# The first product of a mixture-of-experts layer in 26 block products instead of 28, with its operands kept in DRAM

## The chip, the core and the metric

One core of a Trainium2 chip runs the whole program. The metric is device time in microseconds from the start to the end of one execution; shown are the median of the runs and, beside it, one execution that was profiled. PE is the matrix engine (PEld its weight loads), DVE the vector engine, ACT the scalar engine, POOL GpSimd, SP the engine that issues most DMAs.

## The reference, cut to what matters

```python
# chunked attention over q, k, v (4 x 8 x 768 x 64) gives x, 3072 tokens of 512
def _moe_ref(x, w_gate, w1, w2):
    ...                              # P: 3072 x 8, a softmax normalised 8 times over rows and columns
    for e in range(E):               # 8 experts
        h = np.maximum(x @ w1[e], 0.0)      # 512 -> 1024
        ye = h @ w2[e]                      # 1024 -> 512
        out += P[:, e:e + 1] * ye
    return out.astype(np.float32)
```

All is float32, and every token goes through every expert.

## The kernel before, in words

**Tiling.** The tokens are cut in six *units* of 512, each in two halves of 256 (`GT`). The program goes through 48 pairs of expert and unit, `units[n]`: expert 0 on its six units, then expert 1 backwards, and so on. For each pair there is a *first product* (`hidden`, L1616), `h = relu(x @ w1)`, and a *second* (`output`, L1867), `h @ w2`, scaled by the routing weight and added to a running output.

**Number format.** Each float32 operand is scaled by a power of two and split in a high and a low float16 part (`split`, L509 to L528: ScalarE writes the high part, VectorE subtracts it for the low part). A block product is three passes, high x high, high x low, low x high (`PASSES`), each a 128x128 weight load and a 256-column matmul.

**Seven products for eight.** The first product is cut by pairs of feature blocks `fp` (four of them), and each is a 2x2 by 2x2 block product done with seven products (Strassen-Winograd). That takes, of each operand, seven blocks: some are the blocks themselves, four are sums of blocks. So a unit has 4 x 7 = 28 products of 6 matmuls, 168 in all. `run` (L1632) issues a product into one of three PSUM banks (`px`, `py`, `pz`); `read` (L1657, ScalarE) copies a bank of 256 columns out, `plus` (L1667, VectorE) adds it to a copy. The second product does the same over 256-column halves of `w2`, with the four sums of relu'd blocks formed on VectorE (`rsum`, L1766), cut in high (L1777, L1802 on ScalarE) and low parts (L1810, L1826 on VectorE; the first eight of L1826 on POOL, as `aside` says). Its matmuls have names `yx`, `yy`, `yz`. Expert 0 takes plain second products (`plain_output`, `yp`, L2126), since the routing isn't known then; unit 0 of expert 0 is plain throughout (`first_unit`, `pp`).

**Operands.** Tokens: attention runs in blocks of 128 tokens (`tq`, `tk`, `sp`, `ta`, `xp`, `xt` are its matmuls and transposes), two blocks make a half `xg`. `build` (L1245) forms the seven blocks of a unit in SBUF (sums by POOL and VectorE), uses them at once for expert 0 and stores them once (`xkeep`, 1792 KB); later experts load each unit's in one DMA, two units ahead. Weights: for each expert and `fp`, `load` brings raw weights, `cut` forms four sums on POOL (L602) and splits them in place; a pass ahead (`maxima`) finds the largest magnitude with VectorE's reduction (L558), from which `scales` makes the factor.

**Output.** `fetch_acc` loads the running output of a tile (`akeep`), POOL adds one part to it (L1931), VectorE adds the scaled PSUM bank (L1941, L1975), SP stores it again; the last expert stores to `out`.

**What sets the order.** `Plan` collects tasks with an engine, a cost and a priority, and `run` (L164) writes each engine's instructions in the order in which its own costs let them start. Where it expects PE to wait over 0.4 us before the attention has ended, `pad` (L126) has PE do filler matmuls on the identity (`warm`, L427) for 0.8 of the gap. Engines run their queues in order; a semaphore holds each instruction until its inputs are there. Up to `LATE` (unit 4) attention and expert 0 are interleaved; from then on the plan has all PSUM banks for the products.

## Time and profile before

| What | Value |
|---|---|
| Median of 2 runs | 1919.92 us (1918.02 to 1921.83) |
| Span of the profiled execution | 1917.9 us |
| PE, DVE, ACT, POOL busy | 99%, 75%, 54%, 27% of the span |
| Matmuls of the first product | 7896 |
| Matmuls of the second product | 7056, and 576 plain ones of 512 columns |
| Filler matmuls | 168 |
| DMA | 254.8 MB, 133 GB/s over the span |

The profiled execution gives its span alone, 1917.9 us from its first to its last instruction; the median of the runs stands 2.0 us above it. Busy times are sums of modelled intervals: a 256-column matmul is listed with 273 ns, though the next starts 109 ns after it. So for PE the count of matmuls in a stretch says more than their durations, and idle time before an instruction is the sign of a wait. A group's line gives its busy time, the mean of one instruction in ns, and the idle time before it with what ended it.

### The profile page before, as it was taken

How to read it: one execution, taken by the hardware profiler on the slowest of the kernel's cores; microseconds unless marked ns; L12 is line 12 of the kernel's file. 1: busy time of each engine (PE TensorE's matmuls, PEld its weight loads, DVE VectorE, ACT ScalarE, POOL GpSimd, SP SyncE). 2: the span in 40 equal slices, each digit the busy share in tenths (PEclk: the TensorE clock that was granted, in tenths of full speed). 3: DMA queues.
4: the chain of work that ended last, by engine and by line, in shares of the span. 5: the costliest groups of instructions: out<-in, count | busy, mean ns of one | idle time of the engine just before them, and what ended most of it. 6: DMA issues, size and time to landing. Idle time of an engine off the chain costs nothing.

```text
span 1917.9 us, 47295 instructions
## 1 busy us (share of the span) xinstructions
PE 1903.2 (99%) x19616; PEld 1641.0 (86%) x19616; DVE 1436.4 (75%) x2396; ACT 1033.6 (54%) x2019; POOL 524.4 (27%) x549
## 2 busy tenths in 40 slices
PE   9999999999999999999999999999999999999999
PEld 7777676688888888888888888888888888888888
DVE  6776569778679866898668875898678885786565
ACT  4765565556456545646445554655555554564453
POOL 1220001544224221432124231342124232332112
PEclk9999999999999999999999999999999999999999
DMA  8678753453235342265214533245313732322321
GB/s 198 174 194 209 171 172 116 129 204 125 83 110 172 127 148 85 78 197 185 92 63 149 197 105 127 78 160 176 138 45 105 242 122 94 100 83 84 127 83 67
DMA packets 246791, 254.82 MB, mean 133 GB/s; under 512 B 113264, under 2 KB 180272, under 8 KB 242224
## 3 DMA queue, kind: packets, MB, share of 16 engines
q1 hardware_dynamic: 244452, 251.21, 41.2%
q8 instruction: 153, 2.51, 0.6%
q10 hardware_dynamic: 2124, 0.59, 0.2%
q14 instruction: 62, 0.51, 0.1%
HBM read 187.84 MB, written 63.44 MB: 131 GB/s over the span
## 4 chain that ended last, share of the span: by engine, by line
PE 96%; DMA 2%; DVE 1%; ACT 0%; issue 0%; SPq 0%; ACTq 0%; DVEq 0%
PE px L1598 26%; PE yx L1598 23%; PE pz L1598 13%; PE yz L1598 11%; PE py L1598 6%; PE yp L2126 6%; PE yy L1598 6%; DMA q<-in_q_dram 1%; PE xp L1137 1%; PE sp L1069 1%; PE pp L2045 1%; PE tq L1006 1%; PE tk L1010 0%; PE ta L1127 0%; PE xt L1178 0%; DVE w L521 0%
## 5 line engine op out<-in xcount | busy, mean ns | idle before, releaser
L1598 PEld LDWEIGHTS <-w 128*128 128x128 f16 x7896 | 771.4, 98 | 91.9 <-issue 0.6
L1598 PEld LDWEIGHTS <-h 128*128 128x128 f16 x7056 | 690.4, 98 | 81.4 <-issue 1.5
L1598 PE MATMUL px<-x,w 128*128 128x256 f16 x4512 | 549.1, 273 | 0.0
L1931 POOL TENSOR_TENSOR acc<-acc,y 128x256 f32<-128x256 f32 x252 | 267.5, 1068 | 862.1 <-ACT y L1906 842.7
L1598 PE MATMUL yx<-w,h 128*128 128x256 f16 x4032 | 467.5, 273 | 1.3 <-DVE acc L1941 1.3
L1657 ACT ACTIVATE q<-px 128x256 f32<-128x256 f32 x376 | 142.8, 381 | 294.2 <-PE px L1598 289.5
L1598 PE MATMUL pz<-x,w 128*128 128x256 f16 x2256 | 278.2, 273 | 0.0
L1598 PE MATMUL yz<-w,h 128*128 128x256 f16 x2016 | 233.8, 273 | 0.0
L1826 DVE TENSOR_TENSOR h<-ss,h 128x1024 f16<-128x1024 f32 x160 | 215.0, 1346 | 4.0 <-ACT h L1802 3.5
L1777 ACT ACTIVATE h<-c 128x768 f16<-128x768 f32 x168 | 140.8, 838 | 106.4 <-DVE c L1667 106.4
L1802 ACT CAST h<-ss 128x1024 f16<-128x1024 f32 x168 | 174.1, 1039 | 20.4 <-DVE ss L1766 19.6
L1766 DVE SCALAR_TENSOR_TENSOR ss<-c,ss 128x256 f32<-128x256 f32 x336 | 168.3, 501 | 8.2
L1810 DVE SCALAR_TENSOR_TENSOR h<-c,h 128x768 f16<-128x768 f32 x168 | 165.3, 984 | 9.2 <-ACT h L1777 9.1
L1667 DVE SCALAR_TENSOR_TENSOR c<-px,q 128x256 f32<-128x256 f32 x188 | 78.0, 422 | 103.2 <-PE px L1598 94.9
L1906 ACT ACTIVATE y<-yx,pscale 128x256 f32<-128x256 f32 x168 | 79.4, 473 | 114.8 <-PE yx L1598 110.6
L1598 PE MATMUL py<-x,w 128*128 128x256 f16 x1128 | 139.2, 273 | 0.0
L2126 PE MATMUL yp<-w,h 128*128 128x512 f16 x576 | 132.0, 379 | 0.0
L1667 DVE SCALAR_TENSOR_TENSOR c<-py,q 128x256 f32<-128x256 f32 x188 | 78.5, 422 | 60.2 <-PE py L1598 56.7
L1766 DVE SCALAR_TENSOR_TENSOR ss<-c,h 128x512 f32<-128x512 f32 x168 | 120.8, 719 | 3.1 <-ACT h L1754 3.0
L1598 PE MATMUL yy<-w,h 128*128 128x256 f16 x1008 | 116.9, 273 | 0.0
L2126 PEld LDWEIGHTS <-h 128*128 128x128 f16 x576 | 56.0, 98 | 57.9
L513 ACT ACTIVATE w<-ws,sw 128x1024 f16<-128x1024 f32 (+1 forms) x64 | 69.3, 1089 | 65.5 <-POOL ws L602 65.5
(158 smaller groups left out, 1773.0 us busy)
## 6 DMA issues: line engine op xcount, KB each, us to landing
x<-xkeep SPq DMA_DIRECT2D x28, 1792.0 KB
akeep<-acc SPq DMA_DIRECT2D x168, 256.0 KB
acc<-akeep SPq DMA_DIRECT2D x168, 256.0 KB
w1f<-in_moe_w_dram SPq DMA_DIRECT2D x72, 256.0 KB
w2f<-in_moe_w_dram SPq DMA_DIRECT2D x32, 512.0 KB
w1fm<-in_moe_w_dram SPq DMA_DIRECT2D x56, 256.0 KB
w2fm<-in_moe_w_dram SPq DMA_DIRECT2D x28, 512.0 KB
xkeep<-x SPq DMA_DIRECT2D x6, 1792.0 KB
```

What stands on the lines that cost most here:

```text
L513: lambda: nc.scalar.activation(dst(0), src(), AF.Copy, scale=s),
L1598: nc.tensor.matmul(dst.t, a, b, start=(not more and n == 0), stop=(n == end), skip_group_check=more,)
L1657: lambda: nc.scalar.activation(t.t, src.t, AF.Copy, scale=DOWN),
L1667: lambda: nc.vector.scalar_tensor_tensor(c.t[:, o], src.t, DOWN, q.t, op0=ALU.mult, op1=ALU.add),
L1766: lambda: nc.vector.scalar_tensor_tensor(dst(), src(), 0.0, other(), op0=ALU.max, op1=op),
L1777: lambda: nc.scalar.activation(h.t[:, 0, 0:3], c.t, AF.Relu),
L1802: lambda: nc.scalar.copy(h.t[:, 0, 3:7], ss.t),
L1810: lambda: nc.vector.scalar_tensor_tensor(h.t[:, 1, 0:3].rearrange("p a n -> p (a n)"), c.t.rearrange("p a n -> p (a n)"), 0.0, h.t[:, 0, 0 ...
L1826: lambda: spare.tensor_tensor(h.t[:, 1, 3:7], ss.t, h.t[:, 0, 3:7], op=ALU.subtract),
L1906: (lambda: nc.scalar.activation(t.t, src.t, AF.Copy, scale=f))
L1931: lambda: nc.gpsimd.tensor_tensor(acc.t[:, cols], acc.t[:, cols], q.t, op=ALU.add),
L2126: nc.tensor.matmul(py.t, hf.t[:, hl, where[fh], o : o + P], room(fp, WIDE * wl + DM * fh, WIDE * wl + DM * (fh + 1)), start=(fp == 0 and i ...
```

## The change

**26 products.** The first product of a unit is one product of a 4x4 block matrix (four feature blocks by four contraction blocks) and a 4x2 one (four contraction blocks by two token halves), done with 26 block products where the plain way has 32 and the kernel before has 28. The tables `PRODUCTS`, `X_SUMS` and `W_SUMS` say which sums of blocks are multiplied, and to which outputs each product goes with which sign. It is done for both groups of four feature blocks at once: a product is 2 x 3 matmuls into the two halves of one 512-column PSUM bank, 156 matmuls a unit. Six banks ("lanes" A, B, C, E, D, G) run on from product to product; after a product its bank is read whole, by ScalarE the first time an output is touched (L1912, 8 a unit) and otherwise by VectorE into `c_all` (L1924, 18 a unit).

**Operands through DRAM.** `build` now makes 18 sums of a unit's blocks on POOL, and splits and stores 24 blocks in six groups of 512 KB (`xkeep[u][k]`); every unit, also of expert 0, loads them group by group in four buffers (`part_x`). Weights of an expert are prepared during the expert before (`prepare1`, 32 sums of 128 columns for each of two groups on POOL; `prepare2`), stored and loaded again (`part1`, `part2`).

**Second product.** Its count of matmuls stays. `h` is laid out by output tile instead of by `fp`; the subtraction that makes the low part of the sums (L2075) runs on POOL, four a unit. From expert 2 on, the running output isn't loaded: VectorE or ScalarE makes the scaled tile, and POOL issues a DMA that adds it in DRAM to `out` (L2273).

**Weight scales from sums.** `total` takes, on ScalarE, the sum of magnitudes of each row in place of VectorE's maximum.

```diff
-    KEEP = 4
+    STEP = 0.6554
+    UNIT = STEP * (len(PRODUCTS) + 28)
     LATE = NU - 2
-    ASIDE = NU + 2
-    STEP = UNIT / 56
+    ASIDE = 99
...
+PRODUCTS = (
+    ("v17", "u13", "A", ((7, 1),)),
+    ("v20", "u10", "B", ((6, -1),)),
+    ("v24", "u14", "C", ((0, -1),)),
+    ("v23", "u15", "E", ((5, 1),)),
+    ("v22", "u1", "A", ((6, 1),)),
...
+    def total(e, fp, which, st, deps, prio):
+
+        def go():
+            flat = st.t.rearrange("p a k f -> p (a k f)" if which == 1 else "p a d -> p (a d)")
+            nc.scalar.activation(
+                flat, flat, AF.Abs, accum_out=mxs[:, e, which - 1, fp : fp + 1]
+            )
+
+        return add("ACT", 1.1, go, deps, prio, [st])
...
-                found.append(most(e, fp, which, st, [ld], prio))
+                found.append(total(e, fp, which, st, [ld], prio))
...
+    def part_x(u, k, at):
+        x = buf("x", xpool, [P, 2, 4, GT], F16, f"x_{u}_{k}")
+        ld = add(
+            "SP",
+            1,
+            lambda: nc.sync.dma_start(x.t.rearrange("p a j n -> p (a j n)"), xkeep[u][k]),
+            [xkept[u, k]],
+            at,
+            [x],
+            dma=1.4,
+        )
+        return x, ld
...
-    def hidden(e, u, fp, hs, use_at, aside, place="h"):
+    def hidden(n, hs, use_at, aside):
...
+        for i, (wn, xn, lane, reads) in enumerate(PRODUCTS):
+            (kw, jw), (kx, jx) = W_AT[wn], X_AT[xn]
+            if kx not in xs:
+                xs[kx] = part_x(u, kx, now[0] - 14.0)
+            (x, xl), (w, wl) = xs[kx], part1(e, kw, now[0] - 16.0)
...
+                for g in range(2):
+                    for j, (a, b) in enumerate(PASSES):
+                        nc.tensor.matmul(
+                            dst.t[:, g * GT : (g + 1) * GT],
+                            w.t[:, g, a, jw],
+                            x.t[:, b, jx],
+                            start=(new and g == 0 and j == 0),
+                            stop=(j == len(PASSES) - 1),
+                            skip_group_check=True,
+                        )
...
+                        lambda to=to, dst=dst, by=by: nc.vector.scalar_tensor_tensor(
+                            to(), dst.t, by, to(), op0=ALU.mult, op1=ALU.add
+                        ),
...
+                spare = nc.gpsimd if aside and (t or e > 1) else nc.vector
+                slo = add(
+                    "POOL" if aside and (t or e > 1) else "DVE",
+                    2.3 if aside and (t or e > 1) else 1.3,
+                    lambda h=h, ss=ss, r=r, q=q, spare=spare: spare.tensor_tensor(
+                        h.t[:, 1, q], ss.t[:, r], h.t[:, 0, q], op=ALU.subtract
+                    ),
...
-            dst = out[T * P : (T + 1) * P] if e == E - 1 else akeep[T]
+            dst = out[T * P : (T + 1) * P] if e > 0 else akeep[T]
+            op = ALU.add if e > 1 else None
+            eng, queue, cost = ("POOL", nc.gpsimd, 2) if e > 1 else ("SP", nc.sync, 1)
+
+            def store(a=a, dst=dst, cols=slice(0, DM)):
+                if op is None:
+                    queue.dma_start(dst, a.t)
+                else:
+                    queue.dma_start(dst[:, cols], a.t[:, cols], accum_op=op)
```

**The order, first on PE where unit 1 begins.** `tq`, `tk`, `sp` are attention of later blocks, `yp` plain second products of unit 0, `px` and `pA` the first products of unit 1. Before:

```order
L1006 MATMUL tq_2012<-ident,q_1810 128x128 x4
L2126 LDWEIGHTS h_1_880
L2126 MATMUL yp_1991<-w_0_1_1151,h_1_880 128x512
...
L2126 MATMUL yp_1991<-w_0_2_360,h_2_974 128x512
L1598 LDWEIGHTS w_0_0_650
L1598 MATMUL px_1_0_2049<-x_2005,w_0_0_650 128x256
```

Now:

```order
L1388 MATMUL sp_2776<-kC,qT_2676 32x64 x32
L1325 MATMUL tq_2809<-ident,q_2542 128x128 x4
L1329 MATMUL tk_2828<-ident,k_2579 128x128 x4
L592 LDWEIGHTS ident
L592 MATMUL warm<-ident 128x256
...
L1879 LDWEIGHTS w_0_0_1566
L1879 MATMUL pA_1_2950<-x_0_2848,w_0_0_1566 128x256
```

Unit 1 used to start among the outputs of unit 0; now the queries and keys of blocks 12 and 13 are turned ahead of it, and 81 fillers stand directly before it. Between the last transposes of unit 1's tokens and that first product there are 131 fillers; in the whole program 491, where there were 168.

**VectorE in a steady unit** (expert 4, in its first product; `c` or `c_all` are the output blocks, `ss` the rectified sums, `pr_all` and `ws_all` prepared weights). Before:

```order
L1667 SCALAR_TENSOR_TENSOR c_2_0_16098<-py_2_0_16079,q_4_2_0_16077 128x256
L1766 SCALAR_TENSOR_TENSOR ss_1_3_16106<-c_1_3_15979,h_1_3_16063 128x2x256
L1667 SCALAR_TENSOR_TENSOR c_2_1_16115<-py_2_1_16090,q_4_2_1_16087 128x256
L1810 SCALAR_TENSOR_TENSOR h_1_3_16063<-c_1_3_15979,h_1_3_16063 128x768
L1766 SCALAR_TENSOR_TENSOR ss_1_3_16106<-c_1_3_15979,ss_1_3_16106 128x256 x2
L1826 TENSOR_TENSOR h_1_2_16042<-ss_1_2_16074,h_1_2_16042 128x1024
L1667 SCALAR_TENSOR_TENSOR c_2_0_16098<-px_2_0_16053,q_4_2_0_16136 128x256
```

Now:

```order
L1924 SCALAR_TENSOR_TENSOR c_all<-pC_2_16191,c_all 128x512
L1924 SCALAR_TENSOR_TENSOR c_all<-pE_2_16204,c_all 128x512
L1924 SCALAR_TENSOR_TENSOR c_all<-pD_2_16317,c_all 128x512
L686 SCALAR_TENSOR_TENSOR pr_all<-ws_all,sw,pr_all 128x1024
L1924 SCALAR_TENSOR_TENSOR c_all<-pG_2_16331,c_all 128x512
L1924 SCALAR_TENSOR_TENSOR c_all<-pD_2_16317,c_all 128x512
L1924 SCALAR_TENSOR_TENSOR c_all<-pA_2_16171,c_all 128x512
L1924 SCALAR_TENSOR_TENSOR c_all<-pG_2_16331,c_all 128x512
```

A read of a lane is twice as wide and there are 18 for 12; the subtraction L1826 has left this queue.

**POOL in the same unit.** Before, the additions to the running output:

```order
L1931 TENSOR_TENSOR acc_6_15977<-acc_6_15977,y_4_1_0_16219 128x256
L1931 TENSOR_TENSOR acc_7_16003<-acc_7_16003,y_4_1_1_16240 128x256
L1931 TENSOR_TENSOR acc_6_15977<-acc_6_15977,y_4_1_0_16288 128x256
L1931 TENSOR_TENSOR acc_7_16003<-acc_7_16003,y_4_1_1_16306 128x256
L1931 TENSOR_TENSOR acc_4_16020<-acc_4_16020,y_4_1_0_16329 128x256
L1931 TENSOR_TENSOR acc_5_16072<-acc_5_16072,y_4_1_1_16346 128x256
```

Now:

```order
L2075 TENSOR_TENSOR h_6902<-ss_2_16434,h_6902 128x1024 x2
L780 TENSOR_TENSOR ws_all<-w2f_2_16198 128x256
L780 TENSOR_TENSOR ws_all<-ws_all,w2f_2_16198 128x256
...
L2273 DMA out_dram<-acc_6_16476 128x512
L780 TENSOR_TENSOR ws_all<-w2f_2_16198,ws_all 128x256
L2273 DMA out_dram<-acc_7_16492 128x512
L2075 TENSOR_TENSOR h_6172<-ss_2_16574,h_6172 128x1024
L2273 DMA out_dram<-acc_4_16576 128x512
```

The additions are gone from this queue; the subtractions of the second product's low parts and the DMA issues, each of which waits for its output tile, have come in.

## The prediction

> **What bounds the kernel now.** I read the page first, then the busy time by stretches, then the groups by line and shape, and last short pieces of the timeline. Page and stretches:

> ```profile
> span 1917.9 us, 47295 instructions
> PE 1903.2 (99%) x19616; PEld 1641.0 (86%) x19616; DVE 1436.4 (75%) x2396; ACT 1033.6 (54%) x2019; POOL 524.4 (27%) x549
> ```
> ```profile
> core 0: us, PE busy (x) PEld busy (x) DVE busy (x) ACT busy (x) POOL busy (x), PEclk, DMA share, GB/s
> 0.00:100.00 100.00, 93.10 (x1740) 72.22 (x1741) 67.89 (x120) 60.67 (x117) 19.63 (x30) 1.00 0.75 184
> 100.00:200.00 100.00, 96.75 (x1692) 72.44 (x1691) 68.04 (x125) 59.37 (x124) 10.74 (x15) 1.00 0.81 201
> 200.00:300.00 100.00, 99.97 (x1608) 69.92 (x1607) 62.53 (x133) 59.49 (x120) 13.19 (x15) 1.00 0.57 158
> 300.00:400.00 100.00, 99.96 (x723) 70.39 (x721) 83.06 (x159) 55.61 (x103) 39.66 (x39) 1.00 0.49 161
> 500.00:1800.00 1300.00, 1300.00 (x11910) 1165.13 (x11909) 1014.43 (x1632) 698.88 (x1360) 381.46 (x397) 1.00 0.37 125
> 585.00:622.00 37.00, 37.00 (x341) 33.13 (x339) 35.33 (x51) 21.91 (x42) 18.40 (x18) 1.00 0.62 205
> ```

> PE is busy in all of 500 to 1800 at a full granted clock: 1300 us over 11,909 matmuls is 109.2 ns each, so a steady unit of 336 matmuls lasts 36.7 us and every matmul left out there is worth 109 ns. Even the stretch in which VectorE is busy 35.33 of 37 us leaves PE full. PE is idle only in the attention stage (6.9 and 3.25 us in the first two rows). Two groups say the same of the whole run: 7896 matmuls of the first product and the 4032 of `yx` waited 0.0 and 1.3 us.

> ```profile
> L1598 PE MATMUL px<-x,w 128*128 128x256 f16 x4512 | 549.1, 273 | 0.0
> L1598 PE MATMUL yx<-w,h 128*128 128x256 f16 x4032 | 467.5, 273 | 1.3 <-DVE acc L1941 1.3
> L427 PE MATMUL warm<-ident 128*128 128x256 bf16 x168 | 22.4, 286 | 1.6 <-POOL ident masks.py:199 1.6
> ```

> **The change on PE.** A unit's first product takes 26 x 6 = 156 matmuls of the same shape instead of 168, in 47 units: 564 x 0.1092 = **-61.6 us**. The new order has 491 filler matmuls where the old has 168 (row above), all 323 more in the attention stage. They are instructions in PE's own queue and take their pitch whether or not something is late: 323 x 0.1092 = **+35.3 us**. These two are counted; the rest has to be bounded.

> **First stage: tokens through DRAM.** Before, unit 1's operands are formed in SBUF by eight sums shared by POOL and VectorE:

> ```profile
> 95.58 0.60 PE L1178 MATMUL xt<-ident,xq 128*128 128x128 f32 x4
> 99.42 0.73 POOL L1298 TENSOR_TENSOR xt<-xg 128x256 f32<-128x256 f32 x1
> 101.90 0.16 DVE L457 RECIPROCAL sx<-ux 128x1 f32<-128x1 f32 x1
> 113.74 1.48 PE L1598 MATMUL px<-x,w 128*128 128x256 f16 x12
> 1.84 4.79 DMA k<-in_k_dram
> ```

> The last transposes of the unit run at 95.6, the scale is there at 102.1 (6.5 us later), the first product at 113.7. Now nine sums on POOL must precede the first group (9 x 0.73 = 6.6), then a split on ScalarE and VectorE (1.1 and 1.3, the 1024-wide rows below), a store and a load; no row shows such a round trip, and I take the 4.8 us of the first `k` load in the chain for each (bounds: 1.6 us, what 512 KB take at the 331 GB/s that 205 at a share of 0.62 make in the last stretch, and 8 us, five such transfers in one queue). That is 6.5 + 6.6 + 2.4 + 9.6 = 25 us from the transposes to the first product, against 18.2 before. The order answers with attention work and 131 fillers (14.3 us) between the two, so most of the lateness is already paid in the +35.3. What can come on top is that a filled gap is longer than its filler. Three groups that often follow a filler show by how much:

> ```profile
> L1006 PE MATMUL tq<-ident,q 128*128 128x128 f32 x96 | 15.0, 279 | 2.4 <-DMA q<-in_q_dram 2.4
> L1127 PE MATMUL ta<-ident,s 128*128 128x128 f32 x96 | 14.6, 275 | 0.9 <-ACT s L1108 0.9
> L1178 PE MATMUL xt<-ident,xq 128*128 128x128 f32 x96 | 14.5, 274 | 0.5 <-DVE xq L1157 0.5
> ```

> They waited 3.8 us, 0.25 for each of the 15 filled places of before; 22 more such places make 5.6, and I take **+6 us**. From both ends: -4 (some of the 10 us that PE idled before 200 is now filled) and +30 (six units late by 5 us). The DMA engines get busier here: 18.9 MB of x stored and 15.7 read back for five units, against 11.0 stored and 4.2 of raw tokens before, with less raw now: about 21 MB more on the 70 of the first four rows, so a mean share of 0.66 becomes 0.8 to 0.85.

> **Steady stage: who could hold PE.** Rows for VectorE, ScalarE and POOL:

> ```profile
> L1089 DVE TENSOR_TENSOR s<-sp,sm 128x512 f32<-128x512 f32 x24 | 16.5, 689 | 0.7
> L1826 DVE TENSOR_TENSOR h<-ss,h 128x1024 f16<-128x1024 f32 x160 | 215.0, 1346 | 4.0 <-ACT h L1802 3.5
> L1766 DVE SCALAR_TENSOR_TENSOR ss<-c,h 128x512 f32<-128x512 f32 x168 | 120.8, 719 | 3.1 <-ACT h L1754 3.0
> L1810 DVE SCALAR_TENSOR_TENSOR h<-c,h 128x768 f16<-128x768 f32 x168 | 165.3, 984 | 9.2 <-ACT h L1777 9.1
> L1941 DVE SCALAR_TENSOR_TENSOR acc<-yx,pscale,acc 128x256 f32<-128x256 f32 x84 | 40.0, 477 | 54.5 <-POOL acc L1931 28.3 <-PE yx L1598 26.2
> L521 DVE SCALAR_TENSOR_TENSOR w<-ws,sw,w 128x1024 f16<-128x1024 f32 x56 | 77.7, 1387 | 23.9 <-ACT w L513 23.9
> L521 DVE SCALAR_TENSOR_TENSOR w<-w1f,sw,w 128x512 f16<-128x512 f32 x28 | 25.9, 926 | 0.0
> L513 ACT ACTIVATE w<-ws,sw 128x1024 f16<-128x1024 f32 x56 | 63.9, 1141 | 65.5 <-POOL ws L602 65.5
> L2148 ACT COPY acc<-yp 128x512 f32<-128x512 f32 x24 | 13.9, 580 | 18.8 <-PE yp L2126 18.4
> L1826 POOL TENSOR_TENSOR h<-ss,h 128x1024 f16<-128x1024 f32 x8 | 18.0, 2253 | 20.6 <-ACT h L1802 20.6
> L602 POOL TENSOR_TENSOR ws<-w1f 128x256 f32<-128x256 f32 x64 | 51.4, 803 | 139.8 <-DVE w L521 76.9 <-DMA w1f<-in_moe_w_dram 44.8 <-DMA v_pair<-in_v_dram 7.3
> ```

> VectorE in a unit: 18 reads of whole banks at 0.69 = 12.4; two low parts of 1536 columns, each twice the 768 row, 3.9; rectified sums 2 x (1.35 + 2 x 0.72) = 5.6; six output collects at 0.48 = 2.9: 24.8 us of 35.4 (324 x 0.1092). The next expert's weights add some 24 us per six units (18 pieces of the first weight 13, 12 of the second 11), spread over four units: up to 32 in the fullest. What left VectorE pays for it: the 1.35 us subtractions (four a unit) and the maxima. ScalarE: eight bank reads at 0.58 of some 18 to 27 us in all. A lane is used again three products (1.96 us) after it is left, so a read of 0.6 to 0.7 fits, if VectorE isn't held by something else. x was one transfer a unit:

> ```profile
> x<-xkeep SPq DMA_DIRECT2D x28, 1792.0 KB
> ```

> Now it is six of 512 KB. An expert moves 18.9 MB of x, 6.3 of outputs, 8.4 of raw weights, 7.1 of prepared ones out and 7.1 back: 48 MB in 212 us or 225 GB/s, where 500 to 1800 shows 125 at a share of 0.37; that is a share of 0.67. The stretch with 0.62 left PE full.

> POOL gets the subtractions, 4 x 2.25 = 9.0 us a unit, 64 weight sums of 128 columns an expert and four accumulating DMA issues a unit. No row shows either of the last two. A 128-column sum lies between 0 and the 0.80 us of 256 columns; on the line through the 256 and 1024 rows it is 0.56. An issue lies between 0 and, taking POOL's slowest operation for a row, 2.25 us; I take 1. A unit with 32 weight sums is then 9.0 + 17.9 + 4 = 31 us of 35.4, where POOL was busy 18.4 of 37 at its fullest.

> The trace shows what POOL's subtraction does to VectorE:

> ```profile
> 398.92 2.13 POOL L1826 TENSOR_TENSOR h<-ss,h 128x1024 f16<-128x1024 f32 x1 [3.01 <-ACT h L1802]
> 398.77 0.75 DVE L1667 SCALAR_TENSOR_TENSOR c<-pz,q 128x256 f32<-128x256 f32 x2
> 399.44 1.90 DVE L1766 SCALAR_TENSOR_TENSOR ss<-c,ss 128x256 f32<-128x256 f32 x1
> ```

> The 256-column sum from two SBUF operands took 1.90 us and ended as POOL did; the two before it, from PSUM and SBUF, took 0.75 together although POOL had begun. So the lane reads are not slowed, but whatever takes two SBUF operands (rectified sums, low parts, splits) waits out the subtraction, and lane reads queue behind it. [...] By this rule the move to POOL gives back part of what VectorE gains. I count it as 0.25 us of PE in each of the 18 units that also prepare weights, **+4.5 us** (bounds 0 and 2.3 us each, the second rival).

> **The end.** The last matmuls are followed by one collect and a store:

> ```profile
> 1914.76 0.48 DVE L1975 SCALAR_TENSOR_TENSOR acc<-yx,pscale,acc 128x256 f32<-128x256 f32 x1 [0.83 <-PE yx L1598]
> ```

> 2.7 us lie between that collect's end and the end of the span. The store is now an accumulating one from POOL; between 0 and another such 2.7, I take **+1**. [...]

> **Sum**, against the profiled span: 1917.9 - 61.6 + 35.3 + 6 + 4.5 + 1 = 1903.1. The median of the runs is 2.0 above that span (1919.92): **1905 us**.

> **Rivals.** (1) The fillers cover all that is late: the three estimated terms are 0 and only the counted ones stay, 1891.6 + 2 = 1894. For it, PE's 100% under a VectorE busy 95%. Against it, every filled gap so far ran on a little.
> (2) VectorE and POOL together become the bound in the units that prepare weights: each of the four subtractions holds a two-operand VectorE instruction for up to 1.90 - 0.4 = 1.5 us, 5.9 a unit, and 32 + 5.9 is 38 us against 35.4. 2.3 us in 18 units: 41 us more, 1905 + 41 = 1946, **slower than before**. It decides from the point where VectorE's sum with its blocked time passes 35.4. POOL gets there too if a short sum costs 0.8 (25.7 + 9.0 + 4 = 38.7). For it, the 1.90 row, and that only eight subtractions ran on POOL before; against it, weight splits can slide into the light units (24.8).
> (3) The trip through DRAM is late in each of the first five units beyond its filler, since two thirds to four fifths of DMA time is taken there: +4 to +8 us each, 1905 + 20 to 40, about 1930. For it, the DMA share of 0.81 at 100 to 200; against it, the transfers are rows of 4 KB, and later products of a unit come at 2.6 us per group.
> That the saving does not arrive at all is no rival: the matmuls are gone from PE's order, and no row has PE waiting in the steady stage.

> **Chances.** Forecast 0.50; (1) 0.15; (2) 0.17; (3) 0.18. The range leaves out the upper half of (2) and little else: from 1889 (the counted terms, with a few us of the old idle time filled) to 1942. 2% (38 us), about what a measurement of this kernel can tell from no change, is 1881.5 and 1958.3: faster needs 12 us of today's idle time gone besides (1), 0.04; slower needs (2) and (3) together or (2) beyond its price, 0.06; within, 0.90.

> **What would show it.** In the steady stage PE stays at 100% with 109.2 ns a matmul; units last 35.4. Fillers show x491, and the first output product of the second expert starts some 41 us later than here (35.3 of fillers, 7.9 less for 72 matmuls, 7.9 more because all of a hidden product, not its first half, now stands ahead of it, 6 of waits):

> ```profile
> 399.96 2.24 PE L1598 MATMUL yx<-w,h 128*128 128x256 f16 x19
> ```
>  For (2): PE waits on `c_all` readers by VectorE, or on `h` from POOL, in the units with weight sums, VectorE above 95% there. For (3): PE waits on `x` from DRAM before 350. The forecast is wrong if steady units last over 36 us, or if that start is later than 470.

## The result, and the profile after

The changed kernel takes 2116.95 us (median of 2116.9 and 2117.01) against 1919.92: a ratio of 1.1022, 95% interval 1.1003 to 1.1042. It is slower by 197 us, where 1905 us in a range of 1889 to 1942 had been forecast. The profiled execution has a span of 2115.0 us against 1917.9. First the head of its page:

```profile
span 2115.0 us, 47524 instructions
PE 1939.5 (92%) x19375; PEld 1638.2 (77%) x19375; DVE 1611.4 (76%) x2164; ACT 1116.7 (53%) x1823; POOL 977.8 (46%) x1055
PE 45%; DVE 16%; issue 13%; DMA 11%; POOL 8%; ACT 5%; SPq 1%; POOLq 0%; DVEq 0%; ACTq 0%
q1 hardware_dynamic: 290212, 377.06, 53.4%
q0 software_dynamic: 21312, 37.76, 12.5%
```

PE runs 241 matmuls fewer, as counted (564 fewer of the first product, 323 more fillers), yet it is busy for only 92% of the span, and the chain that ended last (third line) now runs through VectorE, DMA and POOL for a third of the time.

From here on experts are counted from 1, as in the expectations: expert 1 is the one that the kernel and the part ahead of the prediction call expert 0, and expert 8 is the last. To see where the time went, the span is cut at the first output product of expert 2, which starts at 399.96 us before and at 487.2 after. The busy time by stretches, of the kernel before:

```profile
0.00:400.00 400.00, 389.79 (x5757) 284.97 (x5758) 281.52 (x534) 235.14 (x462) 83.23 (x98) 1.00 0.65 176
400.00:1918.00 1518.00, 1513.37 (x13862) 1355.98 (x13859) 1154.84 (x1863) 798.50 (x1559) 441.21 (x452) 1.00 0.36 121
```

And of the changed kernel (length of the stretch, then busy time of PE, PEld, VectorE, ScalarE and POOL, PE's clock, DMA share and GB/s):

```profile
0.00:487.00 487.00, 440.79 (x6078) 321.82 (x6079) 337.33 (x611) 257.80 (x462) 164.46 (x234) 0.96 0.73 214
487.00:2115.00 1628.00, 1498.69 (x13299) 1316.35 (x13297) 1274.10 (x1554) 858.92 (x1361) 813.31 (x822) 0.98 0.65 193
```

The first stage is 87 us longer. The steady stage, from there to the end, is 110 us longer although the trace has 563 matmuls fewer in it: at 109.2 ns each its matmuls need 1452 us of the 1628, so PE loses 176 us there, where it lost 4 of 1518 before. The waits of the changed kernel (total, times, longest) say for what:

```profile
PE pA L1879 <- ACT c_all L1912: 81.9, 37, 5.5
PE pA L1879 <- DMA x<-xkeep: 27.3, 9, 7.4
ACT h L2066 <- DVE ss L1999: 174.1, 98, 4.1
ACT ss L1981 <- POOL h L2075: 51.8, 34, 3.4
```

PE waits for ScalarE's first reads into `c_all`, and for `x`. Summed from the starts of the matmuls after 500 us, 98 of 164 us lost stand ahead of a unit's product 5, the second one of lane A, which needs ScalarE's read of product 1, and 21 ahead of product 18. The output products lose nothing: 18.3 us in nearly every unit. In front of ScalarE's reads stands its cast L2066, which waits for VectorE's L1999, and these sums take twice what they took (719 ns for 512 columns before, L1766). The groups by line and shape, changed kernel:

```profile
L1999 DVE SCALAR_TENSOR_TENSOR ss<-c_all,ss 128x512 f32<-128x512 f32 x168 | 243.9, 1452 | 0.9
L1999 DVE SCALAR_TENSOR_TENSOR ss<-c_all,ss 128x1024 f32<-128x1024 f32 x84 | 107.4, 1278 | 66.0 <-ACT ss L1989 65.5 <-POOL ws_all L867 0.4
L2075 POOL TENSOR_TENSOR h<-ss,h 128x1024 f16<-128x1024 f32 x152 | 367.3, 2423 | 469.8 <-ACT h L2066 412.9 <-issue 28.2 <-PE yx L1840 19.5
```

The 512-column sums take 1452 ns, longer than the 1024-column ones: a sign that something else than their size sets them. The timeline of one unit of expert 8, which prepares no weights and loses 1.8 us like each of its kind, shows it. VectorE, POOL, ScalarE and PE (start, duration, idle time before it in brackets):

```profile
1828.17 0.68 DVE L1999 SCALAR_TENSOR_TENSOR ss<-c_all,ss 128x512 f32<-128x512 f32 x1
...
1829.17 2.98 DVE L1999 SCALAR_TENSOR_TENSOR ss<-c_all,ss 128x512 f32<-128x512 f32 x1
```
```profile
1829.17 2.43 POOL L2075 TENSOR_TENSOR h<-ss,h 128x1024 f16<-128x1024 f32 x1
```
```profile
1832.19 1.04 ACT L2066 CAST h<-ss 128x1024 f16<-128x1024 f32 x1 [2.87 <-DVE ss L1999]
1833.14 0.47 ACT L2236 ACTIVATE acc<-yx,pscale 128x256 f32<-128x256 f32 x1
1833.51 0.59 ACT L1912 ACTIVATE c_all<-pA 128x512 f32<-128x512 f32 x1
```
```profile
1829.70 0.82 PE L1879 MATMUL pA<-x,w 128*128 128x256 f16 x6
...
1834.14 0.82 PE L1879 MATMUL pA<-x,w 128*128 128x256 f16 x6 [1.66 <-ACT c_all L1912]
```

The same sum takes 0.68 us alone and 2.98 while POOL subtracts. ScalarE's cast waits for it, an output copy and the lane reads stand behind the cast, so the read of product 1 (on PE from 1829.70) starts only at 1833.51, and product 5 is held up by 1.66 us. The sum was held for 2.3 us; by that much sooner, the read would have come in time.

### The profile page after: what moved, and what is told of

Read it like the earlier page. It is cut to its first block, busy times and chain, and to the rows that moved or that the text cites. A ratio compares the mean times of both kernels' runs of the same rounds, so it can differ in the third digit from the quotient of the medians.

```text
span 2115.0 us, 47524 instructions
## 1 busy us (share of the span) xinstructions
PE 1939.5 (92%) x19375; PEld 1638.2 (77%) x19375; DVE 1611.4 (76%) x2164; ACT 1116.7 (53%) x1823; POOL 977.8 (46%) x1055
## 3 DMA queue, kind: packets, MB, share of 16 engines
q8 instruction: 152, 2.49, 0.5%
## 4 chain that ended last, share of the span: by engine, by line
PE 45%; DVE 16%; issue 13%; DMA 11%; POOL 8%; ACT 5%; SPq 1%; POOLq 0%; DVEq 0%; ACTq 0%
DVE ss L1999 8%; PE yx L1840 6%; PE pA L1879 6%; PE pB L1879 6%; DMA x<-xkeep 5%; PE pC L1879 4%; PE yp L2401 3%; PE pE L1879 3%; PE yy L1840 3%; PE pG L1879 3%; POOL h L2075 3%; PE pD L1879 3%; POOL ws_all L867 2%; DVE pr_all L686 2%; PE yz L1840 2%
## 5 line engine op out<-in xcount | busy, mean ns | idle before, releaser
L2075 POOL TENSOR_TENSOR h<-ss,h 128x1024 f16<-128x1024 f32 x152 | 367.3, 2423 | 469.8 <-ACT h L2066 412.9
L1999 DVE SCALAR_TENSOR_TENSOR ss<-c_all,ss 128x512 f32<-128x512 f32 (+1 forms) x252 | 351.3, 1394 | 66.9 <-ACT ss L1989 65.5
L1879 PE MATMUL pA<-x,w 128*128 128x256 f16 x1692 | 241.6, 281 | 122.5 <-ACT c_all L1912 81.9
L2066 ACT CAST h<-ss 128x1024 f16<-128x1024 f32 x168 | 174.9, 1042 | 174.4 <-DVE ss L1999 174.1
L1879 PE MATMUL pB<-x,w 128*128 128x256 f16 x1692 | 242.7, 282 | 0.0
L1924 DVE SCALAR_TENSOR_TENSOR c_all<-pA,c_all 128x512 f32<-128x512 f32 x188 | 128.8, 685 | 108.8 <-ACT c_all L1912 60.5
L2273 POOL DMA_DIRECT2D out_dram<-acc x148 | 134.5, 1110 | 118.0 <-DVE acc L2181 115.0
L686 DVE SCALAR_TENSOR_TENSOR pr_all<-ws_all,sw,pr_all 128x512 f16<-128x512 f32 (+2 forms) x126 | 148.9, 1188 | 28.4 <-ACT pr_all L678 27.9
L2047 DVE SCALAR_TENSOR_TENSOR h<-c_all,h 128x1536 f16<-128x1536 f32 x84 | 165.0, 1965 | 0.8 <-ACT h L2010 0.6
L1879 PE MATMUL pC<-x,w 128*128 128x256 f16 x1128 | 164.2, 285 | 0.7 <-ACT c_all L1912 0.7
L1879 PE MATMUL pE<-x,w 128*128 128x256 f16 x1128 | 159.8, 279 | 1.1 <-ACT c_all L1912 0.9
L1912 ACT ACTIVATE c_all<-pA 128x512 f32<-128x512 f32 x94 | 55.7, 593 | 197.3 <-PE pA L1879 196.8
L1924 DVE SCALAR_TENSOR_TENSOR c_all<-pB,c_all 128x512 f32<-128x512 f32 x188 | 128.9, 686 | 8.8 <-PE pB L1879 8.5
L1981 ACT ACTIVATE ss<-c_all 128x512 f32<-128x512 f32 x84 | 52.7, 627 | 144.7 <-DVE c_all L1924 77.7
L1924 DVE SCALAR_TENSOR_TENSOR c_all<-pG,c_all 128x512 f32<-128x512 f32 x141 | 97.1, 689 | 37.7 <-PE pG L1879 37.7
```

Of the source, the lines that this page charges most:

```text
L686: lambda: nc.vector.scalar_tensor_tensor(dst(1), src(), s, dst(0), op0=ALU.mult, op1=ALU.subtract),
L1879: nc.tensor.matmul(dst.t[:, g * GT : (g + 1) * GT], w.t[:, g, a, jw], x.t[:, b, jx], start=(new and g == 0 and j == 0), stop=(j == len(PAS ...
L1924: lambda to=to, dst=dst, by=by: nc.vector.scalar_tensor_tensor(to(), dst.t, by, to(), op0=ALU.mult, op1=ALU.add),
L1999: lambda: nc.vector.scalar_tensor_tensor(dst(), src(), 0.0, other(), op0=ALU.max, op1=op),
L2047: lambda h=h, part=part, flat=flat: nc.vector.scalar_tensor_tensor(flat(h.t[:, 1, 0:3]), part(0, 3), 0.0, flat(h.t[:, 0, 0:3]), op0=ALU.ma ...
L2066: lambda h=h, ss=ss, r=r, q=q: nc.scalar.copy(h.t[:, 0, q], ss.t[:, r]),
```

## Experiments

Theory H is this reading: POOL's subtraction holds VectorE's sums, and the hold reaches PE through the single buffers `ss` and `c_all` and the order on ScalarE. Its rivals are the load of the weight preparation (W) and data that come late from DRAM (D). Each experiment is one timed run unless a range stands with it; the kernel before took 1918 to 1925 us beside them. The first stage varies a little by itself: in the runs whose edit acts only later, the first output product of expert 2 starts between 481 and 491 us.

**The subtraction shortened.**

```diff
-  spare.tensor_tensor(h.t[:, 1, q], ss.t[:, r], h.t[:, 0, q], op=ALU.subtract)
+  spare.tensor_tensor(h.t[:, 1, q.start, 0], ss.t[:, r.start, 0], h.t[:, 0, q.start, 0], op=ALU.subtract)
```

> POOL's subtraction of the low parts (h<-ss,h, 128x1024, 2.42 us each) is done on 128 of the 1024 columns for experts 3 to 8; the rest of those low parts is left as an earlier unit wrote it. The order of every engine stays the one of the changed kernel. In it the first products of these 36 units lose 145 us of PE time (4.5 us a unit in experts 3 to 7, 1.8 in expert 8). Theory H (the subtraction on POOL holds VectorE's two-operand sums and, through the single buffers ss and c_all, the next unit's first lane reads): L1999 falls from 1394 ns mean to about 1000, the wait of product 5 for ScalarE's read nearly goes, and the time falls by 100 us or more, to 1990 to 2020. Rival W (the weight preparation loads VectorE, ScalarE and POOL too much whoever subtracts): only the 1.8 us of an expert without preparation go, some 65 us, about 2050. Rival D (x and weights streamed from DRAM arrive late): no change, 2105 to 2120.

Measured: 2034.18 us, 83 less. The groups by shape:

```profile
L1999 DVE SCALAR_TENSOR_TENSOR ss<-c_all,ss 128x512 f32<-128x512 f32 x168 | 136.3, 811 | 0.9
```

The 512-column sums fall from 1452 to 811 ns with the same order on every engine, the loss at product 5 from 98 to 18 us, and expert 8's units lose nothing but in one. H holds in the place and is short in size (83 of 100), because product 18 now loses 44 us, where 21 were lost. That is the wait for x:

```profile
PE pA L1879 <- DMA x<-xkeep: 50.0, 15, 7.4
PE pA L1879 <- ACT c_all L1912: 13.9, 7, 3.6
```

**The subtraction on VectorE.**

```diff
-        aside = n < len(units) - 1
+        aside = False
```

> The low parts are subtracted by VectorE in every unit (1.3 us in the planner's costs, as in the kernel before) instead of POOL; the planner orders anew. Theory H: no POOL subtraction holds VectorE any more, L1999 falls to 0.7 and 1.35 us per form, ScalarE's reads come in time; VectorE gets 152 x 1.25 = 190 us of work and loses some 115 us of holding: 1980 to 2040. Rival W: VectorE is the full engine in units that prepare weights and gets fuller: 2117 or more. Rival D: no change, 2105 to 2120.

Measured: 2059.9 us. The 512-column sums take 763 ns. VectorE has 190 us more of its own subtraction, and is still busy for 1607 us, as in the changed kernel (1611): what VectorE saved by giving this work to POOL it had spent being held.

**Small loads of x.** From expert 3 on each load moves 256 of 2048 columns.

```diff
-  nc.sync.dma_start(x.t.rearrange("p a j n -> p (a j n)"), xkeep[u][k])
+  nc.sync.dma_start(x.t.rearrange("p a j n -> p (a j n)")[:, 0:256], xkeep[u][k][:, 0:256])
```

> From expert 3 on, each load of x from DRAM moves an eighth of its bytes (the rest of the buffer keeps the operands of an earlier load, so products are of wrong operands); number and order of loads, queues and instructions stay. Theory H: the loads were in time but for a few us, 2090 to 2117. Rival D: PE's waits for x (27 us on PE and 27 on its weight loads in the whole span) and the DMA share of 0.68 were what delayed the units: PE's stalls of 145 us in experts 3 to 8 fall by half or more, to 2045 or less.

Measured: 2077.59 us, between the two. The waits at product 5 stay (93 us), those at product 18 go (21 to 0.5). So the bytes of x cost up to 39 us, a second cause and not the main one; 35 of them arise in the steady stage (1592.5 us for 1627.9), 4 ahead of the first small load.

**Both.** The two edits together.

> POOL's subtraction on an eighth of its columns and x loads of an eighth of their bytes together, from expert 3 on. One by one they took 83 and 39 us off 2116.95. If both are causes of their own, the sum is 1995 or somewhat less, since the stalls at product 18 that stood at 44 us with the short subtraction were waits for x: 1980 to 1997. If they hide each other, 2034 or little less. What then remains over 1920 lies in the first stage and expert 2.

Measured: 1987.04 us, 130 less than the changed kernel, where the single effects add to 122. They are two causes, and they do not hide each other.

**No weight preparation.** Experts 3 to 8 read expert 2's blocks again (`wkeep[e + 1] = wkeep[1]`, and so on; `maxima`, `prepare1`, `prepare2` left out).

> Experts 3 to 8 use expert 2's prepared weights and scales, read again from DRAM: the loads of raw weights, the sums for scales, the weight sums on POOL, their splits and stores are left out after expert 2; the first and second products, x loads, and POOL's subtractions stay. Theory H: the holding subtraction is still there, as in expert 8, which prepares nothing: 1.8 us a unit are left, and 80 us go, 2030 to 2045. Rival W: with the load gone the stalls of these units go altogether, 1970 to 1985. Rival D (DMA traffic of the preparation delays x): between, with the waits for x gone first.

Measured: 2053.15 us, 8 over what H gave. Of the 36 units of experts 3 to 8, 27 now lose 1.8 us each, as expert 8's do, and most of the others wait for x. W falls as a cause of its own: with the whole load gone the stall is still there. In the changed kernel the units of experts 3 to 7 lose 4.5 us each; ahead of product 5 it is 2.35 on average, against 1.8, and the rest is waits for x, a halved clock after the longer gaps (see the end) and smaller waits.

**The subtraction on POOL in the kernel before.** One part of the change alone.

```diff
-    ASIDE = NU + 2
+    ASIDE = 99
```

> The kernel before with one part of the change alone: its subtractions of low parts (128x1024) go to POOL in all units after the first stage, not only in two. It has three buffers each for ss and c there, the changed kernel one of each. Theory H1 (POOL's instruction itself holds VectorE's two-operand sums, and the lane reads behind them, whatever the buffers): the 28-product kernel stalls as the changed one does, 2 to 5 us in each of 40 units, 2000 or more. Theory H2 (the hold is long only because one buffer each of ss and c_all lets nothing run ahead: the next tile's chain waits for POOL's end and the next unit's first reads for the chain): with buffers to spare PE hardly notices, 1915 to 1940.

Measured: 1949.15 us, between the two and nearer to H2: 29 us lost in 40 units, 0.7 each. The groups by shape, in the kernel before and in this run:

```profile
L1766 DVE SCALAR_TENSOR_TENSOR ss<-c,ss 128x256 f32<-128x256 f32 x336 | 168.3, 501 | 8.2
L1766 DVE SCALAR_TENSOR_TENSOR ss<-c,ss 128x256 f32<-128x256 f32 x336 | 292.9, 872 | 8.0
```

The sums take 872 ns for 501, so they are held here too, but little of it reaches PE. The kernel has three buffers each of `ss` and `c`; that these make the difference is likely and not shown, since the two kernels differ in more than that.

**Two `ss` buffers.** First on the kernel with small x loads, with room taken from `x` and the copies; then on the changed kernel, with room taken from the second product's weights.

```diff
-    ring("ss", range(1))
+    ring("ss", range(2))
```

> The kernel with an eighth of each x load (2077.6 us), with two ss buffers instead of one; to make room x has three buffers, not four, and the copies p four, not six. POOL still subtracts in full. c_all stays single. Theory H2: the second tile's chain starts without POOL's end, the lane reads come in time, the wait at product 5 (93 us from 500 on) falls to a third, to 1990 to 2020. Theory H1: POOL's instructions hold VectorE as before, and the time stays within 20 us of 2077.6.

> The changed kernel with two ss buffers, made room for by the second-product weights (four buffers, not five; the first quarter of an expert's is loaded with the other three). x keeps its four buffers and the copies their six; POOL subtracts in full. Theory H2 (the one ss buffer ties the second tile's chain to POOL's end): the wait of product 5 (98 us from 500 on) falls to 30 or less and the time by 50 to 80 us, 2035 to 2070; expert 8's units lose nothing. Theory H1 (POOL's hold alone): within 20 us of 2116.95.

Measured: 2193.19 and 2177.48 us, both slower, which neither theory had. Product 5 does what H2 said: its loss falls from 93 to 19 us and from 98 to 27. The first of the two is not a clean trial, since three buffers of x made PE wait 80 us for x. In the second x keeps its four, and its groups and waits show where the stall went:

```profile
L1999 DVE SCALAR_TENSOR_TENSOR ss<-c_all,ss 128x1024 f32<-128x1024 f32 x84 | 162.3, 1932 | 48.9 <-ACT ss L1989 48.9
```
```profile
PE yx L1840 <- DVE acc L2181: 53.6, 32, 2.6
```

With a second buffer the sums of the second tile run beside POOL's subtraction of the first and are held in turn (1278 to 1932 ns), and the collects L2181 of the output products queue behind them: PE waits 53.6 us for these, where it had waited 1.9. `pA`'s waits for x grow too, from 27.3 to 49.3 us. The single buffer had kept these sums and the subtraction apart. To tell whether the second buffer costs by itself, the subtraction was taken off POOL or shortened with two buffers:

> Two ss buffers (as in the run that rose to 2177.5) and every subtraction on VectorE. Theory H1 (with two buffers the second tile's sums run beside POOL's subtraction of the first, are held by it, and outputs' collects queue behind them): without POOL the second buffer is harmless or a gain over the one-buffer run with VectorE (2059.9): 2020 to 2060. Theory N (the second buffer costs by itself, by the weights moved to four buffers or by the planner's other order): 2090 or more.

> Two ss buffers with POOL's subtraction on an eighth of its columns from expert 3 on; the order of every engine is that of the two-buffer run (2177.5). Theory H1: the hold is gone, VectorE's 128x1024 sums fall from 1.93 to 1.3 us, the waits of output products for collects (53.6 us) go, and the time falls by more than the 83 us that the same edit took with one buffer: 2060 or less. Theory N: what the two-buffer run lost stays, 2095 or more.

Measured: 2044.12 and 2044.55 us. Without the hold the second buffer is a gain of 16 with VectorE's subtraction and a loss of 10 with the short one; with the hold it loses 60. In the second of these runs the 1024-column sums are back at 1393 ns, and PE's wait for L2181 is gone. So theory N falls, and it is POOL's instruction that costs, in either arrangement.

**The subtraction in four.** Each piece 128x256 on POOL.

```diff
-  spare.tensor_tensor(h.t[:, 1, q], ss.t[:, r], h.t[:, 0, q], op=ALU.subtract)
+  for m in range(2): for k in (0, 2):
+      spare.tensor_tensor(h.t[:, 1, q.start + m, k:k+2], ss.t[:, r.start + m, k:k+2], ...)
```

> The changed kernel with each subtraction on POOL as four instructions of 128x256 columns, 0.7 to 0.9 us each, so 3 to 3.4 us where one took 2.42; order else the same. Theory H1 (a VectorE sum is held until the end of the POOL instruction in progress): holds are shorter, the 128x512 sums fall from 1.45 to about 1.1 us, though POOL is longer: 2080 to 2115. Theory H2 (the chain through POOL's length and the one ss buffer decides): POOL's part of the chain is longer by 0.6 to 1 us twice a tile, 2125 to 2160.

Measured: 2164.37 us, as H2 had it. The groups of this run:

```profile
L1999 DVE SCALAR_TENSOR_TENSOR ss<-c_all,ss 128x512 f32<-128x512 f32 x168 | 201.0, 1196 | 0.9
L2080 POOL TENSOR_TENSOR h<-ss,h 128x256 f16<-128x256 f32 x608 | 493.2, 913 | 412.1 <-ACT h L2066 391.2 <-ACT y L2166 9.5 <-PE pE L1879 7.0
```

Holds are shorter, as H1 said (1452 to 1196), but four pieces need 3.65 us for 2.42, and the second tile's chain, which waits for POOL's end in the one `ss` buffer, is that much longer: product 5 loses 133 us. So both halves of H act: the hold, and POOL's length within a chain without a spare buffer.

**Late x: order or bytes?** The SP queue holds x loads behind stores of prepared weights that wait for VectorE. In the changed kernel, shortly before a stall of 4.24 us for x:

```profile
1655.62 15.01 SPq L822 DMA_DIRECT2D w2keep<-pr_all  x3
1670.74 2.60 SPq L836 DMA_DIRECT2D w<-w2keep  x4
1673.43 6.32 SPq L993 DMA_DIRECT2D x<-xkeep  x3
```

Three stores hold the queue for 15 us; four loads of second-product weights (896 KB each) and three of x (512 KB) follow within 9 us. The stalled product 18 (from 1691.22) needs the first of these three. It is the second unit of an expert, and the longest stalls for x are in such units. The stores were therefore taken for ready later by the planner:

```diff
-  s.ready = max(s.ready, t.end + late)
+  s.ready = max(s.ready, t.end + late + s.slack)      # slack 10.0 for stores of weights; 8.0 for those of x in the second
```

> The planner takes the stores of prepared weights to DRAM for ready 10 us later than it did, so SP issues x and weight loads ahead of them; nothing else is edited. In the changed kernel these stores waited 334 us in SP's queue for VectorE's splits (L950), with all loads behind them. Theory S (x is late because it stands behind those stores): the waits for x after 500 us go as with an eighth of the bytes, 2065 to 2090. Theory B (bytes): no gain, 2105 to 2130.

> As the run before, and the stores of x are taken for ready 8 us later too, so that the attention's loads of q, k and v go ahead of them in the first stage. Theory S: the first stage ends 10 to 30 us sooner (start of the first output product of expert 2 at 455 to 475), and the whole is 2040 to 2075. Theory B, or if the trip itself is the length of the stage: no sooner or later (x comes 8 us later to its first product), 2085 to 2130.

Measured: 2230.3 and 2270.51 us. The first output product of expert 2 starts at 512.4 and 546.4 us. The stores' wait in the queue falls from 334 to 28 us in the first, but x waits stay (25 us for `pA`), and now the second product's weights come late:

```profile
PE yx L1843 <- DMA w<-w2keep: 122.1, 11, 17.9
PE pA L1882 <- DMA x<-xkeep: 25.2, 6, 6.4
```

Theory S, that x is late because of those stores, gets no support. This does not exclude a share of it, as the order changed elsewhere too.

The trace of the changed kernel shows a third thing that sets a load's time, the four buffers of `x`. SP waits longer for PE to free one of them than for the stores:

```profile
SPq L993 <- PE pE L1879: 405.8, 90, 20.6
SPq L993 <- PE pG L1879: 182.0, 69, 4.8
```

Product 18 is the first to need a unit's fifth group, whose buffer comes free when product 4 ends. In the stall above its load was issued 0.8 us after that, and product 18 could start only 17.8 us later, with the weights ahead in the DMA engines (DMA share 1.06 from 1676 to 1690). Of the eight loads that product 18 waited for, two were issued over 7 us after their buffer was free and took only 6 to 7 us: these, 5 us of the 21, point to order. A fifth buffer of `x` was not tried.

**The first stage.** x's way through DRAM at an eighth of its bytes from the start; fillers cut to one in each gap; x's block sums on VectorE (with the small trip); x's preparation 60 us earlier in the planner's priorities.

```diff
-  nc.sync.dma_start(xkeep[u][k], o.t.rearrange("p a j n -> p (a j n)"))
+  nc.sync.dma_start(xkeep[u][k][:, 0:256], o.t.rearrange("p a j n -> p (a j n)")[:, 0:256])   # loads alike
-        for _ in range(n):      # fill
+        for _ in range(1):
-            prepare(X_SUMS, ..., at)
+            prepare(X_SUMS, ..., at, "DVE")
-            expand(at)
+            expand(at - 60.0)
```

> x's way through DRAM moves an eighth of its bytes from the start, in the stores and in the loads (buffers hold zeros elsewhere); queues, order and waits stay. Until the first output product of expert 2 the changed kernel needs 487.2 us, the one before 399.96. Theory B (bytes: the DMA share of 0.6 to 0.9 there delays x, k and weights): this start comes at 450 or earlier and the whole at 2045 or less. Theory S (the loads stand in one queue behind stores that wait for VectorE, and the planner's order stretches the attention around the trip): the start stays at 475 or later, the whole near the 2077.6 of the run with small loads from expert 3 on.

> Each gap in the first stage that the planner fills with idle matmuls gets one of them instead of up to dozens (491 in all, 157 of them before the first work); order, waits and work stay. Theory F (the added fillers are part of what makes the first stage longer, as predicted, 35 us): 2080 to 2095. Theory G (the fillers stand in time in which PE would wait for the operands' trip through DRAM or for VectorE, so they cost nothing): 2110 to 2125, with the gaps now shown as waits for data and a lower clock.

> The kernel with an eighth of x's bytes from the start (2049.7 us, first output product of expert 2 at 459.5), with the 18 block sums of x of each unit on VectorE instead of POOL (0.35 to 0.55 us each against 0.73). Theory P (POOL's 20 us of sums ahead of the trip make the stage longer): this start comes at 430 to 450. Theory V (the length is that of the attention's own chain and of the staging buffers, or VectorE is too full to take them): 455 or later.

> The changed kernel with the preparation of x (block sums, splits, stores) 60 us earlier in the planner's priorities, so ahead of the attention's work wherever its inputs are there. Theory O (x's preparation waits its turn in the planner's order): the first hidden product comes before 145 us (158 in the changed kernel), the first output product of expert 2 at 470 or earlier, the whole at 2100 or less. Theory C (the chain through sums, splits, two staging buffers and DRAM sets it, whatever the order): within 8 us of 487 and of 2117, or later because the attention is pushed back.

Measured: 2049.67, 2111.78, 2079.4 and 2119.91 us; the first output product of expert 2 starts at 459.5, 484.3, 466.8 and 486.8 us (487.2 in the changed kernel). Of the 87 us, 28 go with the bytes, between what B and S gave. Without most of the fillers the stage is 3 shorter, which is within the scatter and far from 35, so they stand in time in which PE would have waited (theory G). Sums on VectorE bring no gain (7 later, V), and priorities change nothing (C). The remaining 59 are not laid to one cause by these runs. What the trace shows is where they arise: the logits of the last unit (`lq`) come at 340 us instead of 287, and the eight rounds of routing that follow take 55 us instead of 31, from the first column sum to the last.

**Combined.** Subtraction on VectorE, two `ss` buffers, x asked for earlier.

```diff
-  xs[kx] = part_x(u, kx, now[0] - 14.0)
+  xs[kx] = part_x(u, kx, now[0] - 34.0)
```

> Subtractions on VectorE, two ss buffers (2044.1), and x's loads asked of SP 20 us earlier. If the waits for x of that run (34 us, product 18 in an expert's last units) are SP's order, 2010 to 2030; if they are stores that stand ahead in the queue and wait for VectorE, or bytes, 2035 to 2055. In neither case does it beat the kernel before: the first stage keeps its 87 us, and the 564 matmuls are worth 61.6; 1.04 to 1.07 of its time.

Measured: 2046.89 us (2046.38 to 2053.17), ratio 1.0656, 95% interval 1.0634 to 1.0678. Asking earlier gains nothing (2044.1 without it), and PE still waits 36 us for x. Eight of the ten loads that product 18 waited for were issued 0.2 us after PE had freed their buffer, so that asking could not bring them sooner; they then took 9 to 15.5 us. So what is left here is bytes ahead of them together with the four buffers, not SP's order. No version of the 26 products reached the kernel before; the nearest, 1987.04 us, leaves out seven eighths of the subtraction and of x's loads from expert 3 on.

## Why the prediction was wrong, point by point

The working made the stretch from expert 2's first output product to the end 1462 us long (1903.1 less 441); it took 1628. Of these 166 us, 124 go with the two edits together (1627.9 to 1503.9 us), and 18.5 are lost in expert 2, where neither acts; the other 23 are not laid to a cause. The first stage took another 46 us more than foreseen (487.2 for 441).

- **Matmuls, -61.6.** Right in count and rate, and realised in small part: with both edits the steady stage lasts from 481.2 to 1985.2 us, 1504 against 1518. So 14 of the 61 us arrive even then, and 52 us of the stage are still waits, expert 2's 18.5 included.
- **Fillers, +35.3.** Counted right (491), and wrong as a price. "They take their pitch whether or not something is late" is true of the instruction (from one filler's start to the next it is 109 ns in the median), but removing all but 32 of them gave back 3 us of the stage, within the scatter. They were a sign of gaps that were there, not a cost beside them.
- **First-stage waits, +6, bounds -4 and +30.** This step failed in size. The 22 more filled places were 17 (32 gaps in all, by the run with one filler in each, against 15), which makes little. Its own yardstick was 25 us from unit 1's last transposes to its first product, against 18.2; it is 44.8. Single lines of the changed kernel's timeline (PE, POOL, SP's queue, PE):

```profile
113.67 0.60 PE L1497 MATMUL xt<-ident,xq 128*128 128x128 f32 x4
```
```profile
114.97 0.73 POOL L867 TENSOR_TENSOR xt<-xg 128x256 f32<-128x256 f32 x1 [15.73 <-ACT xg L1503]
...
133.67 1.18 POOL L867 TENSOR_TENSOR xt<-xg 128x256 f32<-128x256 f32 x1
```
```profile
138.33 0.36 SPq L1553 DMA_DIRECT2D xkeep<-pr_all  x1
...
150.83 1.21 SPq L993 DMA_DIRECT2D x<-xkeep  x2
```
```profile
158.43 1.44 PE L1879 MATMUL pA<-x,w 128*128 128x256 f16 x6 [7.41 <-DMA x<-xkeep]
```

  The sums end 20 us after they began, since splits and their two staging buffers come between. Store and load took 20 us, not 9.6: twelve of them lie between the store's issue and the load's, in a queue that also issues the attention's inputs. That round trip is the term that was mis-sized. The whole stage is 87 us longer for 41, and its end at 487.2 lies beyond the 470 that was named as the sign of a wrong forecast; of the 87, 28 go with x's bytes, while the cause of the rest stays open.
- **VectorE held by POOL, +4.5, bounds 0 and 41.** This is the step that failed. The mechanism was seen, with its row (1.90 us for a sum of 256 columns; it does not end as POOL does, but 0.29 us later, at 401.34 against 401.05), and its price was put on VectorE's sum of busy time: it was to cost only in the 18 units that prepare weights, and only from the point where VectorE's sum passes the unit's time. VectorE is busy only 1274 of 1628 us in the steady stage, and the hold costs 1.8 us also in units that prepare nothing (expert 8's last 37.2 us, where over 36 was named as the sign). The price belongs on the chain ss, POOL's subtraction, ss of the second tile, cast, ScalarE's queue, first lane read, product 5. Shortening the subtraction gave 83 us back and doing it on VectorE 57, where the second rival, which had the same mechanism and the same wrong condition, gave 41 (its own 37.9 against 35.4 makes 2.5 us a unit and 45 in all, not 2.3 and 41).
- **The lane argument.** "Used again three products after it is left" was right for the read's own 0.6 us and left out what must precede the read: `c_all` and `ss` have one buffer each now, and ScalarE reads in the order of its queue. The kernel before has three of each, and there the same move to POOL costs 29 us, against 57 here (2116.95 for 2059.9).
- **x in the steady stage, 0.** The DMA share was estimated at 0.67 and measured at 0.65, and still x came late, above all in the second unit of an expert: 35 to 39 us by the run with small loads. A mean share does not tell of bursts, nor of how far ahead four buffers let a load be issued. Rival 3 had the mechanism, in the first stage alone.
- **The end, +1, bounds 0 and 2.7.** The stretch from the last collect to the end went from 2.7 to 5.9 us: +3.2, beyond the upper bound.

## What to carry to other kernels

Before a two-operand instruction is moved to POOL, look at what VectorE runs beside it and at how many buffers lie between the held instruction and PE: the same move cost 29 us in the kernel with three buffers and 57 in the one with single ones. Price a hold along the chain that frees the next buffer, not against an engine's busy share; an engine at 78% can be what everyone waits for. When products are saved by reducing buffers and streaming operands, count for each single buffer who must be done before its next writer, and take fillers in a planned order for a forecast of waits.

## What the runs showed of the hardware

A held sum ended shortly after POOL's instruction: the one above took 2.98 us for 0.68 and ended 0.55 us after POOL (1832.15 against 1831.60), and the mean is 1196 ns with pieces of 913 ns on POOL against 1452 with whole ones of 2423. In the whole trace of the changed kernel, 47 of its 512-column sums began during such a subtraction: they took 2.50 to 3.00 us, where those with no subtraction beside them took 0.68 in the median, and all ended 0.55 or 0.56 us after it. Seven low parts that began during one took 3.68 to 3.71 us (1.86 in the median without it), 17 splits of 512 columns 2.26 us in the median (0.75 without it). Of the lane reads, which take one operand from PSUM, 57 began during one and took 0.67 to 0.69 us, 0.69 in the median as without it.

Gaps on PE cost twice here. After product 13 of one unit had waited 2.49 us, the timeline and the stretches of the changed kernel show (six matmuls a row; PE's clock is the third number from the end):

```profile
1682.54 1.00 PE L1879 MATMUL pB<-x,w 128*128 128x256 f16 x6
1683.33 1.48 PE L1879 MATMUL pC<-x,w 128*128 128x256 f16 x6
1684.61 1.48 PE L1879 MATMUL pE<-x,w 128*128 128x256 f16 x6
```
```profile
1684.00:1686.00 2.00, 2.00 (x11) 1.40 (x10) 0.96 (x2) 0.00 (x0) 0.00 (x0) 0.50 1.06 345
```

An accumulating store of 256 KB occupied POOL for 1.11 us on average (estimated at 1), and took 6.7 us in the median from issue to landing.

```profile
L2273 POOL DMA_DIRECT2D out_dram<-acc x148 | 134.5, 1110 | 118.0 <-DVE acc L2181 115.0 <-ACT acc L2236 2.3 <-issue 0.4
out_dram<-acc POOLq DMA_DIRECT2D x140, 256.0 KB, 6.7
```
